# A fused attention, mixture-of-experts and MLP kernel: in each attention round x's copy goes first on ScalarE, then the state's copy and the first step on W, and W's raw pieces begin a round later

## The chip, the cores and the metric

The kernel runs on one core of a Trainium2 chip. The core has a matrix engine (TensorE, PE in the profile, with its weight loads as PEld), VectorE (DVE), ScalarE (ACT), GpSimd (POOL) and SyncE (SP), which here issues the transfers. Each engine runs its own instructions in program order, and the engines wait for one another by semaphores. The metric is the device time of one execution in microseconds.

## The reference: what is computed

Three stages follow one another. The first is a linear recurrence over 768 steps for 4 batches of 8 heads with 48 dimensions:

```python
cur = np.einsum('bhd,bhe->bhde', u[None] * kt, vt)
y[:, :, t] = np.einsum('bhd,bhde->bhe', rt, state + cur)
state = w[None, :, :, None] * state + np.einsum('bhd,bhe->bhde', kt, vt)
```

Its output, 3072 tokens of 384 numbers, is x. Tokens whose skip score is positive go to the best of 8 experts (a two-layer MLP, 384 to 1024 to 384), and their result is weighted and added. The last stage is `((x @ w1) * (x @ w2)) @ w3 @ w_out`. w3 and w_out don't depend on x, so the kernel forms their product W = w3 @ w_out once, while the recurrence runs.

## The kernel before

The recurrence is cut into 24 tiles of 128 tokens; a tile is a chunk of 64 steps for two of the batches, and two tiles (`bp` 0 and 1) make up a chunk of all four. The loop `for n in range(NT - 2)` (L807 to L847) issues one round for each tile. A round n computes the factors FK of tile n+2 (`prep`, DVE L384), the scores of tile n+1 (`scores`, PE L396), masks them into Fs (`evac`, DVE L401), puts the bonus on the diagonal (`bonus`: a reduce into z, DVE L420, and a copy_predicated into Fs, DVE L421), and then the output y of tile n (`y_mm`, PE L442 for the part inside the chunk and L445 for the state's part). y is copied to x (`x_out`, ACT L463) and stored; x of tile n-1 is transposed (`x_trans`, PE L473) and copied to xT (ACT L475), from which a round later the routing logits come (L486, L489). `ds_mm` (PE L458) adds to the state S, which stays in PSUM. `state_copy` multiplies S by the decay where a pair of chunks ends (DVE L430; tiles 4, 5, 8, 9, ...) and copies it to Ss (ACT L432) for the next y. z lies in the same PSUM bank as S, so the copy of S and the reduce into z are kept in the program's order. `prep_k` and `prep_m` (POOL L408, L414, L415) make kd and m.

Beside this, W is built. Its 13 jobs are four pieces of w_out (768 KB each) and eight of w3 (1024 KB each), in the order `o0, w3_0, o1, o2, o3, w3_1, ...`. The numbers come as 64-bit floats, read as pairs of 32-bit integers into `raww` (two buffers, L103, issued on SP), and are cut down to 32 bits. The generator `w_steps` (L657 to L713) gives three steps for a job: one with the join of job i (DVE L140), the issue of the load of job i+2 and the magnitude of job i+1 (ACT L111); one with the cast hi of job i (ACT L683) and low_bits of job i+1 (ACT L117); one with the remainder lo of job i (DVE L690) and signs of job i+1 (ACT L122). hi and lo are called wo_h, wo_l, w3h and w3l. PE's W matmuls (`keep`, L747) use them, and where there are none yet, dummy matmuls (L277) stand in their place.

The order is written by hand: the loop's body is the order of each engine, and the table `WN` says for each round how many of W's steps are taken at three places in it, the first at the round's top, the second behind x_trans, the third at the round's end. `fresh` is a list by which the kernel keeps, when the instructions are written out, which of W's pieces PE may use from which place of the program on. `state_copy` and the first of W's steps stand at the round's top, before scores; the first two raw loads are issued in rounds 0 and 1, each held until the mask of that round's scores (`copied`).

Of the kernel before, what the change touches and what calls it, by code (L numbers as in the profile page):

```python
# [15 lines left out]
ALU = mybir.AluOpType  # L16
# [4 lines left out]
P = 128  # L21
NB, NH, NS, HD = 4, 8, 768, 48
# [23 lines left out]
W3B = 3  # L46
NFIRST = 18
WK = [(1, 1)] * 9 + [(1, 2)] * 13
WN = [(0, 0, 0)] * 2 + [(1, 1, 1)] * 5 + [(1, 0, 1)] * 15
KW = 16  # L50
NRING = 8
RG = 3
# [11 lines left out]
def fused_kernel(ctx, tc, att, kv, wt, u, wg, we, w3, wo, w12, r, k, v, wu, out):  # L64
    nc = tc.nc
# [29 lines left out]
    def load_wide(pool, tag, src, ahead=2, gate=None):  # L95

        k = src.shape[1]
        if not wide:
            raw = pool.tile([P, k], F32, tag=tag, name=tag, bufs=ahead)
            dma = nc.sync.dma_start(out=raw, in_=src)  # L100
        else:
            raw = pool.tile([P, k, 2], I32, tag=tag, name=tag, bufs=ahead)
            dma = nc.sync.dma_start(out=raw.rearrange("p n w -> p (n w)"), in_=src.bitcast(I32))  # L103
        if gate:
            gate(dma)
        return raw
# [106 lines left out]
    def load_expert(e, q):  # L213
        raw = stg[(4 * e + q) % 3 // 2].tile([P, 2, 2 * D], F32, name="raw")
        nc.sync.dma_start(out=raw, in_=we[e, :, 2 * q:2 * q + 2, :])
        return raw
# [30 lines left out]
    with tc.manual_schedule():  # L247
# [6 lines left out]
        Ss = [ac.tile([P, NH, HD], F32, name=f"Ss{bp}") for bp in range(2)]  # L254
# [3 lines left out]
        def load_t(n):  # L258
            nc.sync.dma_start(out=TB[n % 3].rearrange("p a h t -> p (a h t)"), in_=att[n])
# [40 lines left out]
        def load_w(i, gate=None):  # L300
            if i < len(jobs):
                kind, q = jobs[i]
                raw_w.append(load_wide(nrp, "raww", wo[:, 2 * q * D:2 * q * D + 2 * D] if kind == "o" else w3[q], 2,
                                       gate and (lambda dma: behind(dma, gate, "transfers one after the other"))))
# [10 lines left out]
        for i in range(6):  # L315
            wn = pw[:, i - 1] if i else wc
            n = 1 << i
# [4 lines left out]
        w128 = pw[:, 6]  # L322
# [4 lines left out]
        S = [b[:, 0:D].rearrange("p (h d) -> p h d", h=NH) for b in SB]  # L327
# [52 lines left out]
        def prep(n):  # L380

            t = TB[n % 3]
            FK = FK_[n] = wk.tile([P, 2, NH, CH], F32, name="FK", bufs=3)
            return nc.vector.tensor_tensor(out=FK, in0=t, in1=UT[:, n // 2 % 2], op=ALU.mult)  # L384

        def behind(later, earlier, reason="two operands from SBUF each"):

            tc.add_manual_dep(later.ins, earlier.ins.name, mybir.DependencyInfo(
                mybir.DependencyClass.Sync, mybir.DependencyReason.DATA), reason=reason)

        def scores(n):
            FK = FK_[n]
            sc = ps_1.tile([P, 512], F32, tag="sc", name="sc").rearrange("p (h t) -> p h t", h=NH)
            for h in range(NH):
                for m, d in zip(half, dims):
                    nc.tensor.matmul(sc[m, h], FK[d, 1, h], FK[d, 0, h], start=True, stop=True)  # L396
            return sc

        def evac(n, sc):
            Fs = Fs_[n] = wk.tile([P, NH, CH], F32, name="Fs")  # L400
            return nc.vector.tensor_tensor(out=Fs, in0=sc, in1=mask[:, None, :].to_broadcast([P, NH, CH]), op=ALU.mult)  # L401

        def prep_k(n):

            c, bp = divmod(n, 2)
            if c < NC - 1:
                kd = kd_[n] = wk.tile([P, NH, HD], F32, name="kd")
                return nc.gpsimd.tensor_tensor(out=kd, in0=KV[bp][c % 2][:, 1], in1=KU[:, c % 2], op=ALU.mult)  # L408
# [9 lines left out]
        def bonus(n):  # L418
            z = SB[n % 2][:, 464 + NH * (n // 2 % 2):464 + NH * (n // 2 % 2) + NH]
            nc.vector.tensor_reduce(out=z, in_=P_.pop(n), axis=AX.X, op=ALU.add)  # L420
            nc.vector.copy_predicated(Fs_[n], diag[:, None, :].to_broadcast([P, NH, CH]).bitcast(I32),  # L421
                                      z[:, :, None].to_broadcast([P, NH, CH]))

        def state_copy(n):
            c, bp = divmod(n, 2)
            s = S[bp]
            if c == 0:
                return
            if c % 2 == 0:
                nc.vector.tensor_tensor(out=s, in0=s, in1=w128[:, :, None].to_broadcast([P, NH, HD]),  # L430
                                        op=ALU.mult)
            nc.scalar.copy(out=Ss[bp], in_=s)  # L432

        def y_mm(n, tag="y"):

            c, bp = divmod(n, 2)
            v, Fs, FK = KV[bp][c % 2][:, 2], Fs_.pop(n), FK_.pop(n)
            y = G if n % 2 and n < NT - 2 else ps_1.tile([P, 512], F32, tag=tag, name="y")
            yv = y[:, 0:D].rearrange("p (h d) -> p h d", h=NH)
            for h in range(NH):  # L440
                for m in half:
                    nc.tensor.matmul(yv[m, h], Fs[m, h], v[m, h], start=(h == 0), stop=True, skip_group_check=True)  # L442
            for h in range(NH if c else 0):
                for m, d in zip(half, dims):
                    nc.tensor.matmul(yv[m, h], FK[d, 0, h], Ss[bp][d, h], start=False, stop=True,  # L445
                                     skip_group_check=True)
            y_[n] = y
            if n < NT - 2:
                yb[0] = y
# [204 lines left out]
        done, fresh = set(), [[], [], []]  # L654
# [62 lines left out]
        def w_step(k):  # L717
            for _ in range(k):
                next(wprep, None)
# [10 lines left out]
        def w_ready():  # L730
            done.update(fresh[0])
            fresh[:] = fresh[1:] + [[]]
# [44 lines left out]
        sc = scores(0)  # L777
# [29 lines left out]
        for n in range(NT - 2):  # L807
            w_ready()
            if n == NT - 3:
                raws = {q: load_expert(0, q) for q in range(2)}  # L810
            fk = prep(n + 2)
            w_step(WN[n][0])
            state_copy(n + 1)
            sc = scores(n + 1)
            behind(prep_k(n + 1) or prep_m(n + 2), fk)
            if n < NT - 3:
                prep_m(n + 2)
            copied = evac(n + 1, sc)
            if n < 2:
                load_w(n, copied)  # L820
            bonus(n + 1)
            next(more_consts, None)
            w_ready()
            if n == 0:
                for _ in range(NFIRST):
                    dummy(DQ)
            y_mm(n)
            keep(4 * WK[n][0] if n else 0)
            run_todo()
            x_out(n)  # L830
            if n + 4 < NT:
                load_t(n + 4)
            if n > 0:
                x_trans(n - 1)
            keep(4 * WK[n][1] if n else 0)
            w_step(WN[n][1])
            w_evac(0)
            ds_mm(n)
            place_mm(n % 2)
            if n + 4 < NT:  # L840
                load_v(n + 4)
            if n < NT - 3:
                place(3)
            w_step(WN[n][2])
            run_todo(n < NT - 3)
            if n > 0:
                todo.append((logits, (n - 1,)))  # L847

        a, b, g = NT - 2, NT - 1, len(groups) - 1
        w_ready()  # L850
        sc = scores(b)
        todo.clear()
        yb[0] = G
        for i, step in enumerate([
                lambda: (state_copy(b), evac(b, sc), bonus(b), y_mm(a)),
                lambda: (x_trans(a - 1, G), x_out(a), logits(a - 2), route_a(g - 1)),
                lambda: (logits_out(a - 2), nc.scalar.copy(out=slots, in_=SL[1])),
                lambda: (y_mm(b, "sc"), logits(a - 1), route_b(g - 1), x_out(b)),
                lambda: (x_trans(a), logits_out(a - 1), route_c(g - 1)),
                lambda: (x_trans(b, SB[1]), place(4), place(4)),  # L860
                lambda: (logits(a), logits_out(a)),
                lambda: (logits(b), logits_out(b), route_a(g)),
                lambda: (route_b(g), place_rest()),
                lambda: place_all(g, nc.vector),
                lambda: [split_piece(0, q, raws[q // 2], nc.vector) for q in range(RG)]]):
            step()
            if i == 2:
                spare[0] = ps_1.tile([P, 512], F32, tag="y", name="spare")
            for _ in range(TP[i]):
                keep(TK[i])  # L870
                w_step(TW[i])
                w_ready()
                w_ready()
                if TE[i]:
                    w_evac(0)
# [636 lines left out]
```

## Time and profile before

| what | value |
|---|---|
| median of 3 runs | 632.18 us (631.43 to 632.35) |
| the profiled execution, its own time | 633.43 us |
| its span, first to last instruction | 631.7 us |
| mean granted clock of TensorE in it | 0.989 of full |
| PE busy | 609.8 us, 97% of the span |
| DVE busy | 455.6 us, 72% |
| ACT busy | 307.3 us, 49% |
| POOL busy | 141.4 us, 22% |

The span is what the trace holds; the execution's own time has some 1.7 us around it. Times in rows are microseconds from the span's start. PE's high share says little of any one place: it is an average over stages, and a matmul at the lower clock counts as busy too. The rounds of the loop lie between 13.76 and about 158 us.

### The profile page before, as it was taken

Reading aid. Unit: us, or ns where it says so; the run is one execution under the profiler, and the core shown is the slowest. Engines: PE = TensorE matmul, PEld = TensorE weight load, DVE = VectorE, ACT = ScalarE, POOL = GpSimd, SP = SyncE. Lnnn points to the kernel's source line nnn. Section 1 sums busy time; section 2 is a strip of 40 time slices with the busy share of each in tenths; the row PEclk is TensorE's granted clock in tenths of the full one; section 3 lists DMA queues with packets and bytes.
Section 4 is the critical chain, followed back from the end, with each engine's and each line's share of the span. In section 5 each row is a group of like instructions: output and inputs, shape, how many; then the busy total and the mean of one; then the engine's idle time right before and its main releaser. Section 6 shows DMA issues by size and latency. Waiting matters only on the chain.

```text
span 631.7 us, 15256 instructions
## 1 busy us (share of the span) xinstructions
PE 609.8 (97%) x6399; PEld 558.6 (88%) x6399; DVE 455.6 (72%) x807; ACT 307.3 (49%) x581; POOL 141.4 (22%) x143
## 2 busy tenths in 40 slices
PE   8899999999999999999999999999999999999996
PEld 7888889999889999899987989988988988988985
DVE  7676898988577799999956953854863863863770
ACT  1578877653256676666534543442443442442430
POOL 4954546463040232242132300000000000000000
PEclk9897999999999999999999999999999999999998
DMA  8989789766258778877321002002002002000001
GB/s 296 345 290 322 275 305 335 247 215 216 71 184 294 242 255 294 292 241 254 105 70 57 1 19 83 1 17 84 2 18 83 1 18 84 2 17 35 1 2 54
DMA packets 26940, 90.40 MB, mean 143 GB/s; under 512 B 4009, under 2 KB 10729, under 8 KB 25840
## 3 DMA queue, kind: packets, MB, share of 16 engines
q1 hardware_dynamic: 24816, 84.11, 38.5%
q0 software_dynamic: 2048, 5.24, 2.5%
q8 instruction: 52, 0.85, 0.5%
q14 instruction: 24, 0.20, 0.1%
HBM read 77.61 MB, written 12.39 MB: 142 GB/s over the span
## 4 chain that ended last, share of the span: by engine, by line
PE 71%; DVE 14%; DMA 6%; issue 4%; ACT 3%; POOL 1%; SPq 0%; DVEq 0%; ACTq 0%; POOLq 0%
PE po L1276 16%; PE xy L1235 11%; PE za L1235 10%; PE zb L1235 8%; PE hp L962 5%; PE y L981 4%; PE wp L747 3%; DVE elo L91 3%; PE sc L396 2%; PE S L458 2%; DVE hl L966 2%; DMA xr<-xm,sidx 1%; DMA raw<-in_w 1%; PE y L442 1%; DMA raww<-in_w 1%
## 5 line engine op out<-in xcount | busy, mean ns | idle before, releaser
L1217 DVE TENSOR_TENSOR C<-st,za 128x512 f32<-128x512 f32 x47 | 32.3, 688 | 69.7 <-ACT st L1252 69.6
L91 DVE TENSOR_TENSOR elo<-raw,ehi 128x768 fp32r<-128x768 f32 x64 | 60.4, 949 | 3.3 <-ACT ehi L90 3.3
L1276 PE MATMUL po<-pl,W_hi 128*128 128x512 f32 (+1 forms) x152 | 58.1, 383 | 0.0
L1276 PE MATMUL po<-ph,W_hi 128*128 128x512 f32 (+1 forms) x152 | 58.0, 381 | 0.0
L1276 PE MATMUL po<-ph,W_lo 128*128 128x512 f32 (+1 forms) x152 | 57.5, 379 | 0.0
L1252 ACT COPY st<-xy 128x256 f32<-128x256 f32 x47 | 17.6, 374 | 81.8 <-PE xy L1235 81.8
L962 PE MATMUL hp<-xh,ehi 128*128 128x240 f32 x192 | 54.4, 285 | 3.0 <-DVE hl L966 2.8
L90 ACT CAST ehi<-raw 128x768 fp32r<-128x768 f32 x64 | 52.6, 829 | 1.4 <-DMA raw<-in_we 1.4
L1235 PE MATMUL xy<-bxh,w12h 128*128 128x256 f32 x188 | 53.3, 283 | 0.0
L1235 PE MATMUL xy<-bxl,w12h 128*128 128x256 f32 x188 | 53.1, 282 | 0.0
L1235 PE MATMUL xy<-bxh,w12l 128*128 128x256 f32 x188 | 53.1, 282 | 0.0
L962 PE MATMUL hp<-xl,ehi 128*128 128x240 f32 x192 | 52.6, 276 | 0.0
L962 PE MATMUL hp<-xh,elo 128*128 128x240 f32 x192 | 52.3, 274 | 0.0
L1235 PE MATMUL za<-bxh,w12l 128*128 128x512 f32 x141 | 45.1, 320 | 0.0
L1235 PE MATMUL za<-bxh,w12h 128*128 128x512 f32 x141 | 45.0, 319 | 0.0
L1235 PE MATMUL za<-bxl,w12h 128*128 128x512 f32 x141 | 44.7, 317 | 0.0
L981 PE MATMUL y<-ehi,hh 128*128 128x384 f32 (+1 forms) x128 | 43.3, 339 | 0.0
L981 PE MATMUL y<-elo,hh 128*128 128x384 f32 (+1 forms) x128 | 43.2, 338 | 0.0
L981 PE MATMUL y<-ehi,hl 128*128 128x384 f32 (+1 forms) x128 | 43.1, 337 | 0.0
L962 PEld LDWEIGHTS hp<-xh,ehi 128*128 128x128 f32 x192 | 36.0, 189 | 7.7 <-DVE hl L966 7.2
L965 ACT ACTIVATE hh<-hp 128x240 fp32r<-128x240 f32 x64 | 23.7, 370 | 36.0 <-PE hp L962 35.9
L1000 POOL DMA_INDIRECT xm<-yo,sidx x16 | 21.8, 1359 | 84.7 <-DVE yo L997 53.8
(260 smaller groups left out, 1771.6 us busy)
## 6 DMA issues: line engine op xcount, KB each, us to landing
raw<-in_we SPq DMA_DIRECT2D x32, 768.0 KB, 5.2
KV<-in_kv SPq DMA_DIRECT2D x24, 576.0 KB, 5.8
TB<-in_att SPq DMA_DIRECT2D x24, 512.0 KB, 4.6
raww<-in_w SPq DMA_DIRECT2D x8, 1024.0 KB, 7.4
raw<-in_w SPq DMA_DIRECT2D x8, 768.0 KB, 6.9
xm<-xg SPq DMA_DIRECT2D x48, 96.0 KB, 2.9
out<-ob SPq DMA_DIRECT2D x17, 256.0 KB, 2.0
x<-xm SPq DMA_DIRECT2D x20, 192.0 KB, 2.7
```

Source lines behind the costliest of these rows:

```text
L90: nc.scalar.copy(out=hi, in_=raw)
L91: (eng or nc.vector).tensor_tensor(out=lo, in0=raw, in1=hi.bitcast(F32), op=ALU.subtract)
L396: nc.tensor.matmul(sc[m, h], FK[d, 1, h], FK[d, 0, h], start=True, stop=True)
L747: nc.tensor.matmul(ps, a[:, g], b[:, g], start=(g + i == 0), stop=(g == NF - 1 and i == 2))
L962: nc.tensor.matmul(hp, a, b, start=(i == 0), stop=(i == 8))
L965: nc.scalar.activation(out=hh, in_=hp, func=AF.Relu)
L981: nc.tensor.matmul(ys[e, t], a[:, P * t:P * t + ROWS[t]], b[:, D:2 * D], start=(f == 0 and i == 0), stop=(f == NF - 1 and i == 2))
L1000: ins = nc.gpsimd.indirect_dma_start(out=xm[:, :], out_offset=bass.IndirectOffsetOnAxis(ap=sidx[0:n, j, 1:2], axis=0), in_=yo, in_offset=N ...
L1217: nc.vector.tensor_tensor(out=halves(C[:, 0]), in0=st[:, 0:2], in1=halves(za), op=ALU.add)
L1235: nc.tensor.matmul(o, a, m, start=first and i == 0, stop=(i == 2), skip_group_check=True)
L1252: nc.scalar.copy(out=st[:, 0], in_=X)
L1276: nc.tensor.matmul(po, a[:, f, c], b[:, t], start=(i == 0), stop=(i == 3 * NF - 1))
```

## The change

The decay stays at the round's top as `state_decay`. The state's copy and W's first step move behind `x_out` and the issue of TB's load, ahead of `x_trans`. The first two raw loads are issued in rounds 1 and 2 instead of 0 and 1, and `WN` starts W's steps one step later; from round 8 on each step is in the same round as before. One line merges two entries of `fresh`, so that pieces finished at the new place count for PE from the same place as before.

```diff
@@ -46,7 +46,7 @@
 W3B = 3
 NFIRST = 18
 WK = [(1, 1)] * 9 + [(1, 2)] * 13
-WN = [(0, 0, 0)] * 2 + [(1, 1, 1)] * 5 + [(1, 0, 1)] * 15
+WN = [(0, 0, 0)] * 2 + [(0, 1, 1)] + [(1, 1, 1)] * 5 + [(1, 0, 1)] * 14
 KW = 16
 NRING = 8
 RG = 3
@@ -421,15 +421,16 @@
             nc.vector.copy_predicated(Fs_[n], diag[:, None, :].to_broadcast([P, NH, CH]).bitcast(I32),
                                       z[:, :, None].to_broadcast([P, NH, CH]))
 
+        def state_decay(n):
+            c, bp = divmod(n, 2)
+            if c and c % 2 == 0:
+                nc.vector.tensor_tensor(out=S[bp], in0=S[bp], in1=w128[:, :, None].to_broadcast([P, NH, HD]),
+                                        op=ALU.mult)
+
         def state_copy(n):
             c, bp = divmod(n, 2)
-            s = S[bp]
-            if c == 0:
-                return
-            if c % 2 == 0:
-                nc.vector.tensor_tensor(out=s, in0=s, in1=w128[:, :, None].to_broadcast([P, NH, HD]),
-                                        op=ALU.mult)
-            nc.scalar.copy(out=Ss[bp], in_=s)
+            if c:
+                nc.scalar.copy(out=Ss[bp], in_=S[bp])
 
         def y_mm(n, tag="y"):
 
@@ -809,15 +810,14 @@
             if n == NT - 3:
                 raws = {q: load_expert(0, q) for q in range(2)}
             fk = prep(n + 2)
-            w_step(WN[n][0])
-            state_copy(n + 1)
+            state_decay(n + 1)
             sc = scores(n + 1)
             behind(prep_k(n + 1) or prep_m(n + 2), fk)
             if n < NT - 3:
                 prep_m(n + 2)
             copied = evac(n + 1, sc)
-            if n < 2:
-                load_w(n, copied)
+            if 1 <= n < 3:
+                load_w(n - 1, copied)
             bonus(n + 1)
             next(more_consts, None)
             w_ready()
@@ -830,6 +830,9 @@
             x_out(n)
             if n + 4 < NT:
                 load_t(n + 4)
+            state_copy(n + 1)
+            w_step(WN[n][0])
+            fresh[-2:] = [fresh[-2] + fresh[-1], []]
             if n > 0:
                 x_trans(n - 1)
             keep(4 * WK[n][1] if n else 0)
@@ -852,7 +855,7 @@
         todo.clear()
         yb[0] = G
         for i, step in enumerate([
-                lambda: (state_copy(b), evac(b, sc), bonus(b), y_mm(a)),
+                lambda: (state_decay(b), state_copy(b), evac(b, sc), bonus(b), y_mm(a)),
                 lambda: (x_trans(a - 1, G), x_out(a), logits(a - 2), route_a(g - 1)),
                 lambda: (logits_out(a - 2), nc.scalar.copy(out=slots, in_=SL[1])),
                 lambda: (y_mm(b, "sc"), logits(a - 1), route_b(g - 1), x_out(b)),
```

On ACT this is round 3, from W's magnitude or x's copy to W's signs (in the rows, y and G are the outputs y of even and odd tiles, T the transposed x, Ss the copied state, narw and W the two places for W's 32-bit numbers; line numbers after the change are one higher). Before:

```order
L111 ACTIVATE narw<-raww 128x1024
L489 COPY L<-y 128x9
L683 CAST wo_h<-W 128x768
L117 ACTIVATE raww<-raww 128x1024
L432 COPY Ss_116<-S_203 128x384
L463 COPY xg<-G 128x384
L475 COPY xT<-T 128x384
L122 ACTIVATE raww<-raww 128x1024
```

After:

```order
L464 COPY xg<-G 128x384
L433 COPY Ss_116<-S_203 128x384
L111 ACTIVATE narw<-raww 128x1024
L476 COPY xT<-T 128x384
L684 CAST wo_h<-W 128x768
L117 ACTIVATE raww<-raww 128x1024
L122 ACTIVATE raww<-raww 128x1024
```

The copy of the state stood ahead of x's copy and behind W's cast and low_bits; it now follows x's copy at once. W's magnitude, which began the round, stands between it and xT, and the cast and low_bits stand behind xT.

On DVE, rounds 3 and 4, from one FK to the second next. Before:

```order
L384 TENSOR_TENSOR FK<-TB_120,UT 128x1024
L430 TENSOR_TENSOR S_203<-S_203,pw 128x384
L401 TENSOR_TENSOR Fs<-sc,mask 128x512
L420 TENSOR_REDUCE S_203<-m 128x8
L421 COPY_PREDICATED Fs<-diag,S_203 128x512
L690 TENSOR_TENSOR wo_l<-W,wo_h 128x768
L140 SCALAR_TENSOR_TENSOR narw<-narw,raww 128x1024
L384 TENSOR_TENSOR FK<-TB_118,UT 128x1024
L430 TENSOR_TENSOR S_204<-S_204,pw 128x384
L401 TENSOR_TENSOR Fs<-sc,mask 128x512
L420 TENSOR_REDUCE S_204<-m 128x8
L421 COPY_PREDICATED Fs<-diag,S_204 128x512
```

After:

```order
L384 TENSOR_TENSOR FK<-TB_120,UT 128x1024
L427 TENSOR_TENSOR S_203<-S_203,pw 128x384
L401 TENSOR_TENSOR Fs<-sc,mask 128x512
L420 TENSOR_REDUCE S_203<-m 128x8
L421 COPY_PREDICATED Fs<-diag,S_203 128x512
L140 SCALAR_TENSOR_TENSOR W<-W,raww 128x768
L691 TENSOR_TENSOR wo_l<-W,wo_h 128x768
L384 TENSOR_TENSOR FK<-TB_118,UT 128x1024
L427 TENSOR_TENSOR S_204<-S_204,pw 128x384
L401 TENSOR_TENSOR Fs<-sc,mask 128x512
L420 TENSOR_REDUCE S_204<-m 128x8
L421 COPY_PREDICATED Fs<-diag,S_204 128x512
```

Before, the join of a job stood at the round's top, ahead of FK, and lo behind the copy_predicated of the round after; now join and the lo of the same job both stand between copy_predicated and the next FK.

On SP, the issue order of the transfers from round 0 on (TB and KV are the attention's inputs, xm the stored x, raww W's raw pieces). Before:

```order
L103 DMA raww<-in_wo 128x1536
L466 DMA xm<-xg 64x384 x2
L259 DMA TB_119<-in_att 128x1024
L263 DMA KV_0_112<-in_kv 128x1152
L103 DMA raww<-in_w 128x2048
L466 DMA xm<-xg 64x384 x2
L259 DMA TB_120<-in_att 128x1024
L263 DMA KV_0_114<-in_kv 128x1152
L466 DMA xm<-xg 64x384 x2
L259 DMA TB_118<-in_att 128x1024
```

After:

```order
L467 DMA xm<-xg 64x384 x2
L259 DMA TB_119<-in_att 128x1024
L263 DMA KV_0_112<-in_kv 128x1152
L103 DMA raww<-in_wo 128x1536
L467 DMA xm<-xg 64x384 x2
L259 DMA TB_120<-in_att 128x1024
L263 DMA KV_0_114<-in_kv 128x1152
L103 DMA raww<-in_w 128x2048
L467 DMA xm<-xg 64x384 x2
L259 DMA TB_118<-in_att 128x1024
```

The first piece of w_out now comes behind the first TB and KV shown (tile 4), and the first piece of w3 behind the second ones (tile 5), where each stood ahead of them.

## Rows read from the trace of the kernel before

**Rows 1.** The page: PE's busy time, the granted clock by slices, W's raw loads.
```profile
PE 609.8 (97%) x6399; PEld 558.6 (88%) x6399; DVE 455.6 (72%) x807; ACT 307.3 (49%) x581; POOL 141.4 (22%) x143
...
PEclk9897999999999999999999999999999999999998
...
raww<-in_w SPq DMA_DIRECT2D x8, 1024.0 KB, 7.4
```

**Rows 2.** Windows by round: length, busy PE PEld DVE ACT POOL, clock, DMA, GB/s.
```profile
21.64:29.68 8.04, 6.67 (x151) 6.25 (x149) 4.51 (x5) 4.87 (x8) 7.75 (x14) 0.87 1.02 376
49.98:58.93 8.95, 8.95 (x145) 8.42 (x145) 7.00 (x9) 6.70 (x9) 2.98 (x3) 0.62 0.94 323
64.77:70.62 5.85, 5.85 (x149) 5.54 (x147) 5.72 (x10) 3.03 (x4) 3.83 (x3) 1.00 0.90 310
70.62:78.22 7.60, 6.65 (x161) 6.10 (x157) 5.11 (x11) 7.43 (x13) 4.07 (x3) 1.00 0.75 252
84.84:92.50 7.66, 7.01 (x149) 6.41 (x150) 7.60 (x10) 3.73 (x7) 4.82 (x5) 1.00 0.81 282
92.50:158.20 65.70, 65.70 (x1492) 62.17 (x1494) 57.77 (x104) 37.27 (x66) 33.97 (x30) 1.00 0.74 256
```

**Rows 3.** The chain of waits, 0 to 175 us: start, length, what.
```profile
26.17 1.37 issue
...
36.81 1.24 DVE narw L140
38.07 7.43 DMA raww<-in_wo
...
46.56 0.73 ACT wo_h L683
...
48.09 0.36 ACT Ss L432
...
48.84 0.38 ACT xT L475
...
51.06 0.97 DVE narw L140
...
59.64 0.87 ACT narw L111
...
63.10 0.57 DVE S L420
...
64.32 0.95 DVE wo_l L690
65.27 1.14 DVE FK L384
66.41 1.14 DVE narw L140
67.54 0.48 DVE S L430
68.02 0.57 DVE Fs L401
...
69.23 0.73 DVE Fs L421
```

**Rows 4.** The timeline, 29 to 52 us; in brackets idle time before, and releaser.
```profile
30.21 1.23 DVE L384 TENSOR_TENSOR FK<-TB,UT 128x1024 f32<-128x1024 f32 x1 [1.64 <-DMA TB<-in_att]
...
33.12 0.74 DVE L421 COPY_PREDICATED Fs<-diag,S 128x512 f32<-128x512 int32 x1
...
41.63 1.82 DVE L690 TENSOR_TENSOR w3l<-narw,w3h 128x1024 fp32r<-128x1024 f32 x1
...
45.58 0.93 ACT L111 ACTIVATE narw<-raww 128x768 f32<-128x768 f32 x1 [2.69 <-DMA raww<-in_wo]
...
48.56 0.56 DVE L420 TENSOR_REDUCE S<-m 128x8 f32<-128x384 f32 x1 [2.50 <-ACT Ss L432]
...
49.98 1.14 PE L442 MATMUL y<-KV,Fs 64*64 64x48 f32 x32 [1.52 <-ACT xT L475]
```

## Prediction

> **What bounds the kernel now.** I read the page first. PE is busy for 609.8 us of a 631.7 us span, and the line of granted clocks is below full in slices 2 to 4, the attention rounds alone [rows 1]. So only the rounds in which PE waits or runs slowly can give time back. Cut by round (I take a round to begin with its y matmuls, L442), the windows give the size: from 92.50 us on, PE is busy for 65.70 of 65.70 us, and round 8 shows what a round of PE work without a wait costs, 5.85 us [rows 2]. The rounds between 21.64 and 92.50 us are longer: round 2 takes 8.04 us, of which PE is idle 1.37 and runs at a granted clock of 0.87; round 6 takes 8.95 at 0.62; round 9 takes 7.60 with 0.95 idle [rows 2]. All granted clocks lie between two levels, 1.2 and 2.4 GHz, so 0.62 of 8.95 us is 6.8 us at the lower one, which costs half of that, 3.4 us; 0.87 of 8.04 us costs 1.0 us.
>
> The chain of waits tells what those rounds wait for. From 36.81 to 66.41 us it never touches PE: it goes join (DVE L140) to the raw load to ACT's pieces to the next join [rows 3]. The first turn lasts 51.06 - 36.81 = 14.25 us, the second 66.41 - 51.06 = 15.35 us, and each covers two rounds, because the raw tiles have two buffers and load i+2 waits for join i. So the kernel is bound here by a ring of about 7.1 to 7.7 us a round, against 5.85 of PE. The timeline shows how the ring reaches PE: in round 5 W's magnitude (ACT L111) waits 2.69 us for its raw load, the state's copy stands behind it on ACT, the reduce of z waits 2.50 us for that copy, and y(6) starts 1.52 us late [rows 4]. The profile names xT as y(6)'s releaser, but it had been written; the copy_predicated after that reduce is what came last.
>
> **The change part by part.** No operation is added or removed; PE and POOL keep their order. Four things move.
>
> (1) *The first two raw loads go a round later.* Ahead of the transfer TB(5), which FK(5) awaits for 1.64 us at 30.21 [rows 4], stood one 1,024 KB load that now comes behind it (the SP piece above). At the 376 GB/s of that stretch this is 2.8 us. The wait itself is all that FK(5) can gain at once: 1.64. The first join no longer stands before that FK either. So copy_predicated of round 3, which ended at 33.12 + 0.74 = 33.86, ends at about 32.2. Bounds: 33.86 if the load's place makes no difference, 31.0 if all of the 2.8 us shows. PE's idle 1.37 at 26.17, which the chain calls issue [rows 3], falls in the same crowded stretch (DMA share 1.02 [rows 2]); with or without it the scores of round 2 are done before that FK, so I give it nothing.
>
> (2) *x's copy and the state's copy go ahead of W's piece on ACT.* That takes the 2.50 us wait out of the reduce, since a late raw load no longer holds the state's copy, and it takes the state's copy, 0.36, and x's, which has the size of xT's 0.38, out of the old ring [rows 3]. What is now behind the waiting W piece on ACT: x's transposed copy (for whom PE's logits wait a round later), the cast hi, low_bits and signs.
>
> (3) *join and lo of a round both come after copy_predicated, and before the next FK.* This is the new cost. lo waits for the cast hi of the same round, hi stands behind xT and behind the magnitude that may wait for a load, and FK, decay, Fs, reduce and copy_predicated of the next round stand behind lo on DVE. So a one-round ring closes. By the chain's rows [rows 3]: Ss 0.36, magnitude 0.87, xT 0.38, hi 0.73, lo 0.95, FK 1.14, decay 0.48 (half of the rounds), Fs 0.57, reduce 0.57, copy_predicated 0.73: 6.78 with the decay, 6.30 without, either more than PE's 5.85. And the load's ring is still there, now through DVE: join 0.97, load 7.43, magnitude 0.87, xT 0.38, hi 0.73, lo 0.95, FK 1.14, Fs 0.57, reduce 0.57, copy_predicated 0.73: 14.34 us in two rounds, against 14.25 before. The old ring's tail (low_bits, Ss, xg, xT, signs) is exchanged for an equally long one.
>
> (4) *From round 8 on each step is in its old round.* Round 9, whose 0.95 us of idle the old order put behind signs, may lose it; xT now stands behind the piece there, which can cost the logits as much. I take both as nothing, with -1.6 to +1.6 as ends: the waits in rounds 9 and 11 sum to 1.6 (7.60 - 6.65 = 0.95 and 7.66 - 7.01 = 0.65 [rows 2]).
>
> **The sum.** Copy_predicated of round 3 ends at 32.2. To that of round 4: 6.78. Two turns of the load's ring lead to that of round 8: 14.34 and, with the 1,024 KB pieces and the decay, 15.35 as in the second turn before. That is 68.7, and y(9) can start 0.07 behind it: 68.7 against 70.62. I add one lo that is drawn out as the one at 41.63 of before was, 1.82 us [rows 4] where FK of the same 1,024 elements takes 1.14 [rows 3]: 0.68. So y(9) starts at 69.4, 1.2 us earlier, and from there on PE decides as before. The profiled execution took 633.43 us (its span of 631.7 and 1.7 around it): 633.43 - 1.2 = 632.2 us. The median of the runs shown is 632.18, so the profiled one was 1.25 above it, and the forecast is **no change: 632.2 us**. A measurement tells 0.2%, 1.26 us, from no change.
>
> Ends: the earliest copy_predicated (31.0), no stretched lo and the second turn at 14.34 + 0.48 give y(9) at 67.0, 3.6 earlier: 629.8. With copy_predicated at 33.86 and two stretched lo it is 71.8, 1.2 later: 634.6.
>
> **Rules beside rows.** PE's 1.37 us idle is followed at once by 1.2 GHz, and the 1.52 us before y(6) by the 6.8 us of it; the 0.95 us of round 9 is followed by full clock [rows 2 to 4]. The Trainium skill, "TensorE: Matmul & The Clock Gate", section "HAM oscillation", says that waits of PE for transfers, repeated in each iteration, let the clock fall again and again. The trace agrees as far as two such waits go. By that rule a kernel whose ring leaves a gap in every round, as this one's does, falls after the larger gaps: rival B.
> DVE's instructions with two operands are not always of one length: lo of 1,024 elements takes 1.82 us at 41.63, where POOL is at work beside it, and lo of 768 takes 0.95 at 64.32 [rows 3, 4]. The Trainium skill, "GPSIMD Engine Reference", section "Key points", has the two engines share their SBUF interfaces when a DVE instruction has two SBUF inputs. By it, a DVE that runs join, lo and FK in one piece would be met every round: all three lo that lie on the chain (rounds 3, 5 and 7) would be stretched, two more than the sum has, 1.4 us and 633.6 in all. One of the two rows speaks for it and one against, and I give it 0.06, within B's chance.
>
> **The rivals.**
> *A, faster.* The ring turns without collisions, and with the first loads out of the way neither the 1.37 us stall nor a fall of the clock occurs. For it: the two half-clock stretches of before cost 4.4 us between them, and both follow stalls in the stretch where loads crowd. Against: the ring, not PE, set rounds 3 to 8, so most of that was hidden under it. It gives the lower end, 633.43 - 3.6 = 629.8. Chance 0.29.
> *B, slower.* One place: y(7) or y(8), behind the magnitude that waits for its load in the ring of (3). Where PE idles there for 1.4 us or more, as before y(6), the clock falls, and a stretch like that of round 6 costs 3.4 us; the ring hides at most a third of it, since the stretch then reaches into rounds 9 and 10, where PE decides. That leaves 2.3 to 3.4: 632.2 + 2.6 = 634.8. It decides from a ring of 7.3 us a round on (5.85 + 1.45); the sum above has (14.34 + 15.35) / 4 = 7.4, but PE enters round 3 with some slack, as y(3) may start earlier, and the gaps spread over several rounds. Chance 0.32, with D and the rule on POOL in it.
> *C, no change by another way.* W's raw loads simply take as long as before, the DMA's 7.4 us [rows 1] set both rings, and the order on ACT is free. The median's 632.2 again; it is part of my forecast's chance.
> *D, W's parts come too late for PE.* PE's first W matmuls stand in round 6, and the parts for them are finished in rounds 3 and 4. A whole round of slack speaks against it; I give it 0.02.
>
> **How the numbers follow.** My forecast and C together have 0.39, A 0.29, B with D 0.32; these are also the chances for within 0.2%, faster and slower. The range must reach into A and B until a fifth is left out: from a little under A's 629.8, for a round 9 without its wait, 629.4, to 635.5, B with most of its price. The likeliest case alone has 631.0 to 633.5.
>
> **What would show it.** In the profile after, (1) is right if FK(5) starts before 29 us with no wait for TB. (2): no reduce waits for Ss longer than 0.5 us. (3): FK follows lo directly in rounds 4 to 8, the chain runs through join, load, hi, lo, FK and copy_predicated, and these rounds take 7.1 to 7.7 us each. (4): rounds 9 to 11 together lose 1 to 2 us. y(9) should start between 69 and 70 us. I am wrong if the rounds 3 to 8 come down to about 6 us (then the ring was not closed, A), if a half-clock stretch of over 3 us stands anywhere behind 55 us (B), or if the magnitude no longer waits for its loads at all.

## The result, and the profile after

The changed kernel took 635.81 us (median of 4 runs, 634.51 to 636.08) against 631.80 of before (4 runs, 631.25 to 632.35): 1.0058 of it, 95% interval 1.0037 to 1.0078. Repeated with 12 runs against 23, all on one chip, it was 634.25 against 632.74: 1.0029, interval 1.0007 to 1.0051. So the change makes the kernel slower, by 0.3 to 0.6%; the forecast was no change (632.2), and 635.81 lies 0.3 us above its range, 634.25 inside.

Page of the profiled execution after (634.51 us, span 632.8), the rows that answer to [rows 1]:

```profile
PE 610.3 (96%) x6399; PEld 558.9 (88%) x6399; DVE 457.7 (72%) x807; ACT 306.4 (48%) x581; POOL 143.5 (23%) x143
...
PEclk9979799999999999999999999999999999999999
```

Two dips of the clock, again before 92 us and in other slices. The windows by round, columns as in [rows 2]; here rounds 2, 4, 7, 8 and 9, and the later ones:

```profile
21.13:26.87 5.74, 5.74 (x152) 5.32 (x149) 3.22 (x5) 2.24 (x6) 5.53 (x11) 1.00 1.01 364
...
34.03:43.33 9.30, 8.19 (x153) 7.33 (x150) 7.16 (x9) 7.41 (x10) 5.22 (x4) 0.71 0.79 271
...
55.45:62.46 7.01, 6.22 (x149) 5.67 (x146) 4.46 (x7) 5.15 (x8) 2.59 (x4) 1.00 0.93 341
62.46:69.55 7.09, 6.26 (x143) 5.73 (x144) 5.18 (x8) 6.16 (x7) 3.78 (x4) 1.00 0.94 325
69.55:80.33 10.78, 9.75 (x154) 8.70 (x156) 9.07 (x16) 8.84 (x15) 3.76 (x4) 0.68 0.71 253
...
93.42:159.00 65.58, 65.25 (x1476) 61.61 (x1474) 58.48 (x104) 38.09 (x68) 32.18 (x30) 1.00 0.74 258
```

Round 2 has lost its wait and its slow stretch. Rounds 7 and 8 now take 7.0 and 7.1 us, round 4 9.30 (1.11 idle, clock 0.71) and round 9 10.78 (1.03 idle, clock 0.68).

The table of waits shows what was exchanged. First before, over rounds 2 to 11 (engine, tile and line that waited, for what; us in total, times, longest):

```profile
DVE S L420 <- ACT Ss L432: 5.5, 3, 2.5
...
ACT narw L111 <- DMA raww<-in_w: 2.7, 2, 1.8
ACT narw L111 <- DMA raww<-in_wo: 2.7, 1, 2.7
...
ACT W L111 <- DMA raww<-in_w: 2.6, 1, 2.6
```

and after:

```profile
DVE wo_l L691 <- ACT wo_h L684: 9.5, 4, 3.0
ACT Ss L433 <- DVE Fs L421: 7.4, 7, 2.2
...
DVE w3l L691 <- ACT w3h L684: 2.1, 1, 2.1
...
ACT W L111 <- DMA raww<-in_wo: 1.5, 1, 1.5
```

ACT's waits for raw loads, 9.3 us in all before (the three rows shown, and 1.3 in three waits for other pieces), are down to 1.5, and the reduce waits no more for Ss. In their place stand two that did not exist: Ss waits 7.4 us for copy_predicated, lo waits 11.6 for hi (9.5 and 2.1). ACT now waits for DVE in front of work that DVE waits for.

The chain of waits has that ring row by row, as the counterpart of [rows 3]:

```profile
58.84 1.22 DVE FK L384
...
61.63 0.74 DVE Fs L421
62.39 0.48 ACT Ss L433
62.87 1.05 ACT narw L111
63.93 0.36 ACT xT L476
64.29 0.74 ACT wo_h L684
65.09 0.84 issue
65.93 1.22 DVE FK L384
```

From FK at 58.84 to FK at 65.93 it is 7.09 us for one round, with the decay and the magnitude of a 1,024 KB piece; the prediction's terms give 6.78. What the chain calls issue ahead of the second FK is the time of lo, which takes 0.96 us from 65.06 on.

### The profile page after: what moved, and what is told of

Read it like the earlier page. It is cut to its first block, busy times and chain, and to the rows that moved or that the text cites. A ratio compares the mean times of both kernels' runs of the same rounds, so it can differ in the third digit from the quotient of the medians.

```text
span 632.8 us, 15244 instructions
## 1 busy us (share of the span) xinstructions
PE 610.3 (96%) x6399; PEld 558.9 (88%) x6399; DVE 457.7 (72%) x807; ACT 306.4 (48%) x581; POOL 143.5 (23%) x143
## 4 chain that ended last, share of the span: by engine, by line
PE 78%; DVE 11%; DMA 3%; issue 3%; ACT 2%; POOL 1%; SPq 0%; DVEq 0%; ACTq 0%; POOLq 0%
PE po L1279 16%; PE xy L1238 11%; PE za L1238 10%; PE zb L1238 8%; PE hp L965 6%; PE y L984 5%; PE wp L748 4%; DVE elo L91 3%; PE sc L396 3%; PE S L459 2%; PE y L443 1%; PE G L443 1%; PE y L446 1%; PE G L446 1%; DVE hl L969 1%
## 5 line engine op out<-in xcount | busy, mean ns | idle before, releaser
L965 PE MATMUL hp<-xh,ehi 128*128 128x240 f32 x192 | 54.5, 285 | 2.6 <-DVE hl L969 2.4
L1003 POOL DMA_INDIRECT xm<-yo,sidx x16 | 22.6, 1413 | 84.7 <-DVE yo L1000 58.6
```

Of the source, the lines that this page charges most:

```text
L965: nc.tensor.matmul(hp, a, b, start=(i == 0), stop=(i == 8))
L1003: ins = nc.gpsimd.indirect_dma_start(out=xm[:, :], out_offset=bass.IndirectOffsetOnAxis(ap=sidx[0:n, j, 1:2], axis=0), in_=yo, in_offset=N ...
```

## The experiments

Each time stands beside runs of the kernel before on the same chip; a ratio is to those. Runs of one kernel spread over some 6 us here, so the ratios carry the verdicts and the traces the mechanisms.

**The changed kernel again, twice, and the kernel before again.**

> The changed kernel once more, for its spread and a second trace. Three theories. Ring: the ring copy_predicated, Ss, magnitude, xT, hi, lo, FK, Fs makes rounds 6 to 8 seven us long, PE's scores wait 0.6 to 0.7 us for Fs in two of them, and the clock falls behind such gaps. State: in round 8 the copy Ss(9) stands on ACT behind the routing's r_d, so that y(9)'s second part starts 1.0 us late, and the clock falls there. Loads: it is the raw loads, now a round later. Expected by all: 635.8 us, 1.004 to 1.008 of before; y(12) between 93 and 96 us. By ring the scores' waits of 0.6 us or more stand in rounds 7 and 8 again, by state the wait of about 1.0 us before L446 in round 9.

> A third trace of the changed kernel. The sum of PE's waits in rounds 2 to 11 between 4 and 7 us, the clock's loss 3.4, 5.1 or 6.9 us; by state a wait before L446 in round 9 wherever PE reaches it on time; by ring gaps ahead of the scores in rounds 6 to 8.

> The kernel before, a second trace. If the falls of the clock lie at fixed places, at 28 and 51 us again; if they follow chance, elsewhere. Round 2's idle 1.4 us on PE is there again if it belongs to the order of this kernel.

The changed kernel took 634.25 us (12 runs), 635.01 in the single further run; before 633.61 in its single run. What all three theories expected, 635.8 us, 1.004 to 1.008 and y(12) between 93 and 96 us, was missed: it is 634.25 us, 1.0029 and, in the trace of that run, 91.28 us. That gives three traces after and two before. Times are told here from y(0), since the traces begin differently. Before, y(9) comes at 56.86 and 55.71 us, y(12) at 78.74 and 77.49. After, y(9) comes at 56.29, 55.65 and 54.54, y(12) at 80.16, 77.13 and 77.21. So at y(12) the two kernels stand level, at 78.1 us in the mean before and 78.2 after. From y(12) to the end of the span the third trace after takes some 2.8 us more than the other two; 1.49 us of that is one wait of PE in round 17 that the profile calls issue. The second trace of before, rounds 2 and 5:

```profile
21.91:27.78 5.87, 5.74 (x152) 5.32 (x149) 3.07 (x4) 3.72 (x5) 5.66 (x11) 1.00 1.01 372
41.19:50.95 9.76, 8.94 (x145) 7.95 (x147) 7.34 (x9) 6.69 (x9) 3.08 (x4) 0.65 0.78 255
```

Round 2 takes 5.87 us there without the 1.37 us wait and without a slow stretch, and the slow stretch lies in round 5. So the place of the falls, and the wait on which the prediction's reading of round 2 rested [rows 2, 3], change from one execution of the same kernel to the next and don't follow from its order alone. In the traces after, waits of 0.5 us or more before the scores for Fs stand in rounds 7 and 8 in two of three, the wait of 1.0 us before L446 of y(9) in two of three; where PE came late to y(9) for another reason, it was not there. PE's idle time in rounds 2 to 11 was 5.1, 4.3 and 6.0 us after, 5.3 and 5.0 before, and the clock's loss (length times one minus granted clock, by round) 6.9, 3.4 and 1.7 after, 5.1 and 3.4 before; the 6.0 us of waits in the third trace lie in the range that was expected, the 1.7 us do not.

By traces alone the two kernels can't be told apart; it takes the runs. There, the time times one minus the granted clock of each run is an estimate of what the clock takes: over 12 and 23 runs 5.0 us after and 5.2 before in the mean, and what is left is 629.4 against 627.6. **On that chip, by this estimate, the loss of 1.5 to 2 us is in waits and work at full clock, not in falls.** In the first 4 runs the clock took 7.6 us and 627.9 is left; the runs of before that stand beside them have no clock on record. Beside the 627.6 of the larger set those 4 runs point the other way, to falls, so what made up the first distance of 4.0 us isn't known.

**Half of the change: loads and W's steps later, order as before.**

```diff
-WN = [(0, 0, 0)] * 2 + [(1, 1, 1)] * 5 + [(1, 0, 1)] * 15
+WN = [(0, 0, 0)] * 2 + [(0, 1, 1)] + [(1, 1, 1)] * 5 + [(1, 0, 1)] * 14
-            if n < 2:
-                load_w(n, copied)
+            if 1 <= n < 3:
+                load_w(n - 1, copied)
```

> Only the loads and W's steps start later; ACT's order of a round and the place of state copy and of the first W step are those of before. Loads: 635 us or more. Ring and state: not slower than before, 631 to 633, since lo does not stand between hi of the same ring and FK, and Ss keeps its place ahead of r_d.

636.1 us, 1.0043 (1.0023 to 1.0063). By the time, Loads was right and ring and state were wrong. But the run doesn't show the loads apart from the order: the magnitude is now in front of Ss at the round's top, and waits there for its load:

```profile
ACT narw L111 <- DMA raww<-in_w: 5.1, 2, 3.0
...
ACT W L111 <- DMA raww<-in_w: 4.2, 2, 4.0
```

**The other half: the order alone, loads as before.**

```diff
-            if 1 <= n < 3:
-                load_w(n - 1, copied)
+            if n < 2:
+                load_w(n, copied)
...
-WN = [(0, 0, 0)] * 2 + [(0, 1, 1)] + [(1, 1, 1)] * 5 + [(1, 0, 1)] * 14
+WN = [(0, 0, 0)] * 2 + [(1, 1, 1)] * 5 + [(1, 0, 1)] * 15
```

> Only the order: state copy and the first W step behind x's copy, but loads and W's steps begin when they did before, so the first step is the cast hi and low_bits, and the magnitude stands at the round's end. Ring: without magnitude and xT between Ss and hi the ring is 1.2 us shorter, 5.6 plus join, some 6.2: 632 to 633.5. State: Ss(9) is still behind r_d, the wait of 1.0 us in round 9 stays and so does most of the loss: 634.5 to 636. Loads: as before, 631.8.

641.19 us, 1.0128 (1.0103 to 1.0153): all three theories missed. Rounds 4 and 5 take 9.9 and 9.8 us. I had summed the ring through lo and forgot the join, which in this order stands ahead of FK and waits for signs of the same round:

```profile
ACT Ss L433 <- DVE Fs L421: 22.1, 9, 3.6
...
PE sc L396 <- DVE Fs L401: 7.9, 6, 3.4
```

Ss 0.36, hi 0.73, low_bits 0.8, xT 0.4, signs 1.9 to 2.5, join 1.0, FK 1.1, Fs, reduce and copy_predicated 1.9 make 8.2 to 8.8 us. So each half alone loses more than both together: by the ratios 2.7 and 8.1 us against 1.8. Not all of the 8.1 is the ring itself: by the estimate above the clock takes 11.6 us in these runs, against 5.2 before, and in the trace rounds 4 and 5 lose 5.1 us to it, behind the wait of 3.4 us. Starting the loads a round later puts the magnitude, and not low_bits and signs, between Ss and the join; and the new place of W's step takes the late magnitude out from in front of Ss.

**The state's copy ahead of x's copy, and of the routing.**

```diff
             keep(4 * WK[n][0] if n else 0)
+            state_copy(n + 1)
             run_todo()
...
-            state_copy(n + 1)
             w_step(WN[n][0])
```

> The changed kernel with the state's copy issued ahead of the routing's work of the round (behind y's matmuls), so ahead of r_d and of x's copy; all else as changed. State: the wait before L446 in round 9 is gone, 632 to 633. Ring: the ring is the same, 635 to 636. Loads: 635 to 636.

639.17 us, 1.0096 (1.0070 to 1.0122). The wait before L446 in round 9 is gone, as State said, and the time is longer all the same; ring was not hard enough on it:

```profile
ACT Ss L433 <- DVE Fs L421: 22.6, 10, 6.1
DVE wo_l L691 <- ACT wo_h L684: 11.3, 4, 3.7
```

An Ss that comes earlier in ACT's order waits longer for copy_predicated (22.6 us, against 8.3 by the same window after), and x's copy, the magnitude and hi wait behind it.

**Without the edge from copy_predicated to Ss.**

```diff
-            z = SB[n % 2][:, 464 + NH * (n // 2 % 2):464 + NH * (n // 2 % 2) + NH]
+            z = wk.tile([P, NH], F32, name="z", bufs=2)
```

> The changed kernel with z in a small SBUF tile of its own instead of a column range of the state's PSUM bank, so that the state's copy need not wait for copy_predicated. Ring: the edge from copy_predicated to Ss closes the ring through ACT; without it what is left is join 0.97, hi 0.73, lo 0.95, FK 1.14, decay 0.48, Fs 0.57, reduce 0.57, copy_predicated 0.73, 5.7 to 6.1 us, near PE's pace: 1.5 to 3 us faster than the changed kernel, the wait of Ss for Fs gone. Loads: no difference (within 1 us of the changed kernel).

> The kernel before with z in SBUF. If the wait of the reduce for the state's copy behind a late magnitude was what bound it (5.5 us of waits in rounds 5 to 7), 1 to 2 us faster than before. If the ring through the raw load bound it whatever stands behind it, within 0.5 us.

639.05 us with the change, 1.0096 (1.0063 to 1.0129); 635.05 on the kernel before, 1.0030 (1.0005 to 1.0055). Neither the gains that were expected came, nor the equal times of the other theories. The wait of Ss is gone, but z's new place costs more than it gave. Groups of the changed kernel (busy us, mean ns of one, idle before):

```profile
L414 POOL TENSOR_TENSOR m<-KV,un 128x384 f32<-128x384 f32 x11 | 12.0, 1093 | 0.0
...
L421 DVE COPY_PREDICATED Fs<-diag,S 128x512 f32<-128x512 int32 x11 | 8.1, 736 | 0.4
...
L140 DVE SCALAR_TENSOR_TENSOR W<-W,raww 128x768 int32<-128x768 int32 (+1 forms) x4 | 4.3, 1072 | 1.3 <-ACT raww L122 1.3
```

and with z in SBUF:

```profile
L414 POOL TENSOR_TENSOR m<-KV,un 128x384 f32<-128x384 f32 x11 | 15.2, 1380 | 0.0
...
L421 DVE COPY_PREDICATED Fs<-diag,z 128x512 f32<-128x512 int32 x10 | 8.7, 865 | 0.3
...
L140 DVE SCALAR_TENSOR_TENSOR W<-W,raww 128x768 int32<-128x768 int32 (+1 forms) x4 | 5.7, 1422 | 1.2 <-ACT raww L122 1.2
```

copy_predicated takes 865 ns instead of 736, POOL's first product 1,380 instead of 1,093, the join 1,422 instead of 1,072. With z in SBUF a copy_predicated still takes 0.73 us where POOL stands still, and up to 1.14 us beside its products. The experiment took away a wait and added a collision, so it says nothing on the ring.

**lo a round later.**

```diff
-                nc.vector.tensor_tensor(out=lo, in0=x, in1=hi.bitcast(F32), op=ALU.subtract)
-                fresh[-1].append(jobs[i])
+                late.append((jobs[i], lo, x, hi))
+                if not wait_lo[0]:
+                    late_low(fresh[-1])
...
             state_copy(n + 1)
+            late_low(fresh[0])
             w_step(WN[n][0])
```

> The changed kernel with the remainder lo of rounds 3 to 7 a round later on DVE, behind the next copy_predicated and ahead of its join, so that no FK stands behind an instruction that waits for a cast of the same round. Ring: cut; DVE waits for ACT only at the join, rounds 3 to 8 at 5.9 to 6.5 us: 2 to 4 us faster than the changed kernel. Loads: the raw loads still come when they come, no difference within 1 us.

(wait_lo is set around the last step of rounds 3 to 7.) 633.6 us, 1.0026 (1.0004 to 1.0047), beside the changed kernel's 1.0029 and, in its first 4 runs, 1.0058. DVE's waits for ACT in rounds 2 to 11 fall from 12.9 us to 6.3, and the time stays. **So the ring through lo, though the chain shows it, is probably not what costs the most**: beside the larger set the 2 to 4 us that breaking it was to give back don't show, and Loads, which expected no difference, was right. Beside the first 4 runs some 2 us would show; the changed kernel was not run beside this one on the same chip, so this is not settled. PE's idle time in this trace is 5.3 us; what isn't put down to issue stands in rounds 8 to 11 now (0.70, 0.90, 0.86 and 0.33).

**The routing behind the copies, then r_d alone.**

```diff
             keep(4 * WK[n][0] if n else 0)
-            run_todo()
...
             state_copy(n + 1)
+            run_todo()
             w_step(WN[n][0])
```

> The changed kernel with the routing's work of a round (r_d and r_pr on ACT, their partners on DVE) issued behind x's copy and the state's copy instead of ahead of them; PE's order is the same. State: Ss(9) no longer waits for r_d, so no wait before L446 in round 9 or 10, and the changed kernel gains about 1 us of PE waits: 632.5 to 633.5 beside 634.4. If what the change costs lies in rounds 3 to 8, or is spread over many small waits, 634 to 635.

642.78 us, 1.0169 (1.0136 to 1.0203). The logits go with the routing, and they write into the PSUM bank that x's copy reads; issued behind it, they wait for it:

```profile
PE G L487 <- ACT xg L464: 3.7, 3, 2.3
PE y L487 <- ACT xg L464: 3.3, 1, 3.3
```

That spoils the test. The second one moves r_d alone, the other routing steps and the logits staying:

```diff
-            run_todo()
+            held = []
+            run_todo(hold=held)
...
             state_copy(n + 1)
+            for fn, args in held:
+                fn(*args)
+                todo.append((NEXT[fn], args))
             w_step(WN[n][0])
```

> The changed kernel with nothing moved but the routing's exponential r_d on ACT (rounds 8, 14, 18), from ahead of x's copy and the state's copy to behind them; PE, DVE and the logits stay as they were, which the earlier run on the routing did not leave. State: the wait of 1.0 us before L446 of y(9) is gone or under 0.5 us, and the time comes about 1 us nearer to before: 633 to 634 beside 634.4. Ring, or many small waits: that wait goes, but another takes its place by round 11; 634 to 635, the same as the changed kernel.

634.26 us, 1.0036 (1.0008 to 1.0064): no gain that shows, as Ring, or many small waits, had it. Its timeline:

```profile
70.00 0.48 ACT L433 COPY Ss<-S 128x384 f32<-128x384 f32 x1 [0.51 <-DVE Fs L421]
...
71.01 1.13 PE L446 MATMUL G<-Ss,FK 48*64 48x48 f32 x32
...
71.20 0.24 ACT L517 ACTIVATE r_d<-r_d 128x48 f32<-128x48 f32 x1 [0.73 <-DVE r_oh L516]
...
84.03 1.15 PE L396 MATMUL sc<-FK 48*64 48x64 f32 x32 [1.51 <-DVE Fs L401]
```

Ss(9) is copied ahead of r_d, and L446 in round 9 starts without a wait; in round 10 the scores wait 1.51 us for Fs instead. The wait behind r_d is real, and taking it away gave no time back. The three traces of the changed kernel have 0 to 0.74 us of idle PE in round 10; that the 1.51 us are the removed wait, moved on, is not shown.

**The state's copy ahead of W's piece, in the kernel before.**

```diff
-            w_step(WN[n][0])
             state_copy(n + 1)
+            w_step(WN[n][0])
```

> The kernel before with only the state's copy ahead of W's piece at the round's top. Before, cast and low_bits (1.5 us) and any wait in front of them stood ahead of the copy for which the reduce waits. If those waits bind (5.5 us of them in one trace before, 5.9 in the other), 630.5 to 632 beside 632.7. If the ring through the raw load sets the pace whatever stands in front of the reduce, within 0.5 us of before.

638.55 us, 1.0121 (1.0087 to 1.0156), again the other way than expected:

```profile
ACT Ss L432 <- DVE S L430: 8.8, 5, 2.3
```

The copy waits for the decay (DVE L430), and W's cast and low_bits, which before ran in that time, now stand behind it. That holds ACT up for 8.8 us (2.6 before), and the joins wait 6.0 us for signs (3.2 before). Yet this trace reaches y(12) at 78.31 us from y(0), no later than those before (78.74 and 77.49). What it lost lies behind the loop: some 5 us at 1.2 GHz between 160 and 180 us, slice 11 of its line of clocks. In the loop, a wait of 2.36 us in round 9 is followed by full clock:

```profile
PEclk9999999999699999999999999999999999999999
...
76.92 0.42 PE L458 MATMUL S<-KV,kd 64*48 64x48 f32 x9 [2.36 <-issue]
```

So that the copy's wait on ACT makes this kernel slower is not shown. Over its 6 runs the clock takes 9.9 us, against 4.7 in the runs before on that chip, and why is open. No kernel of the study beats the one before.

## Where the prediction was right and where it was wrong

**What held.** The ring of (2) and (3): the wait of the reduce for Ss is gone, FK follows lo, the chain runs through magnitude, xT, hi, FK, Fs and copy_predicated, and 7.09 us for a turn stand against 6.78 and, with loads, 7.4. The forecast for y(9), 69.4 - 13.76 = 55.6 us behind y(0), was met in the mean of three traces: 55.5, from 54.5 to 56.3. Rounds 3 to 8 of the profiled execution take 7.1 us in the mean, though singly from 5.9 to 9.3.

**Two of its signs did not hold.** FK(5) starts at 26.83, before 29 us, but still waits 1.12 us for TB. And a half-clock stretch of over 3 us behind 55 us, by which the prediction would call itself wrong and B right, stands in all three traces after: from 72 to 79 us in the profiled one, in round 7 of the second and in round 9 of the third, whose windows follow in this order:

```profile
53.58:63.58 10.00, 9.01 (x150) 8.40 (x147) 5.83 (x8) 7.28 (x12) 5.26 (x4) 0.67 0.92 318
...
68.28:77.56 9.28, 8.24 (x154) 7.23 (x156) 7.74 (x16) 8.15 (x14) 4.87 (x4) 0.82 0.62 216
```

**Two terms up to there were off and cancelled.** The timeline after, counterpart of [rows 4]:

```profile
26.83 1.59 DVE L384 TENSOR_TENSOR FK<-TB,UT 128x1024 f32<-128x1024 f32 x1 [1.12 <-DMA TB<-in_att]
...
29.99 0.73 DVE L421 COPY_PREDICATED Fs<-diag,S 128x512 f32<-128x512 int32 x1
...
33.47 1.75 POOL L415 TENSOR_TENSOR m<-KV,m 128x384 f32<-128x384 f32 x1
...
34.27 2.03 DVE L384 TENSOR_TENSOR FK<-TB,UT 128x1024 f32<-128x1024 f32 x1
```

Copy_predicated of round 3 ends at 30.72, that is 17.46 us behind y(0) (17.48 and 17.48 in the other traces) where the sum had 18.4 and the lower bound 17.2: step (1) was worth 2.6 us against the profiled execution and 2.1 against the second trace of before (19.60). In return FK(6) takes 2.03 us in all three traces, beside POOL's product L415, where 1.14 stood in the sum. The one drawn-out instruction that I took for lo is FK, so y(9) was met partly by luck. The Trainium skill, "GPSIMD Engine Reference", section "Key points", has POOL and VectorE share SBUF interfaces where a DVE instruction has two SBUF inputs; this trace agrees, 2.03 us for FK beside a product of POOL against 1.22 without one, and so does the run with z in SBUF. It isn't always DVE that is held: lo at 33.40 keeps its 0.96 us beside the same product, which takes 1.75 us instead of 1.00. The row that the prediction counted against this, lo at 64.32 before, has no product beside it; the last one ended at 63.18.

**The step that failed**, as far as the traces tell, is the one behind y(9): "from there on PE decides as before", with (4) taken as nothing. From y(9) to y(12) the traces before take 21.9 and 21.8 us, those after 23.9, 21.5 and 22.7, 0.8 more in the mean, in a range that I had put at 1.6 to either side and then set to zero. That takes back the 0.8 us by which these traces reach y(9) earlier than the two before (55.5 against 56.3): it accounts for the gain that didn't come, and the traces don't place the 1.5 us or more that were lost. The spread of the three, 2.4 us, is larger than that mean. A mechanism of it that I had not seen is Ss(9) behind r_d:

```profile
61.18 1.15 PE L396 MATMUL sc<-FK 48*64 48x64 f32 x32 [0.66 <-DVE Fs L401]
...
68.27 1.15 PE L396 MATMUL sc<-FK 48*64 48x64 f32 x32 [0.69 <-DVE Fs L401]
...
70.67 0.24 ACT L517 ACTIVATE r_d<-r_d 128x48 f32<-128x48 f32 x1 [2.03 <-DVE r_oh L516]
...
71.72 1.62 PE L446 MATMUL G<-Ss,FK 48*64 48x48 f32 x32 [1.03 <-ACT Ss L433]
```

Gaps of 0.66, 0.69 and 1.03 us follow in rounds 7 to 9, and the clock is at half from 72 to 79 us. That is rival B's place and price in this one execution. But B as a mechanism is not confirmed: in the third trace after, the same wait of 1.04 us was followed by 1.7 us lost to the clock in its round, and in the second there was no such wait. B's condition, a wait of 1.4 us or more, doesn't part the cases either, as a fall follows 1.03 us here and none the 2.36 us of the last experiment. And the clock's share is no larger than before in the larger set of runs, though it may be in the first 4. The chance for slower, 0.32, was given to falls of the clock; the larger set puts the loss into waits.

**The base was also off.** The sum was set against one execution, with a 1.37 us wait and two slow stretches that it took for the kernel's own. The second trace of before has neither at those places. A gain of 1.2 against an execution that is 1.25 above its median is no gain, which the prediction said; what it did not ask is whether the stall that it saw would come again.

**What stays open.** Three single edges were taken out of the changed kernel: lo ahead of FK, Ss behind r_d, and (with a side effect that spoils it) copy_predicated ahead of Ss. None gave the loss of the larger set back. Nor is there a run that moves the loads and leaves every other wait as it was: each half of the change alone has a wait of its own. Which of the remaining waits carries it isn't settled; that another wait stands behind a removed one, as in round 10 above, was seen, that this is the whole of it was not shown. That the distance was 4.0 us in the first comparison and 1.5 in the second is also open; the clocks of the two sets differ by 2.6 us (7.6 against 5.0).

## What to carry to other kernels

Moving a copy forward on an engine that runs in order helps only if its inputs are ready there: the changed kernel with Ss still further ahead stood 0.96% above the one before, against 0.29% without that move, and Ss held ACT up for 22.6 us instead of 8.3, in front of work that other engines needed. When a move closes a ring between two engines, sum the ring over every instruction between its ends on both, the ones that seem to belong to another step too; the kernel whose join I had left out of the sum stood 8 us above the one before, its falls of the clock included. And take a second trace before reading a stall of one trace as the kernel's own.

## Unexpected in the hardware

PE waits at fixed places of its program for nothing that the profile shows, in most of the kernels here. In the run that moves r_d alone:

```profile
32.48 0.87 PE L459 MATMUL S<-KV,kd 64*48 64x48 f32 x29 [1.07 <-issue]
...
38.41 0.38 PE L277 MATMUL wp<-zb 128*128 128x256 bf16 x2 [1.94 <-issue]
```

The wait ahead of the last 29 S matmuls of round 3 is there in 10 of 14 traces at 32.2 to 33.2 us, from 0.24 to 1.34 us long, and the one ahead of the last 2 dummies of round 4 in 12 of 14, from 0.18 to 2.17. The lengths change from one execution to the next of the same kernel (1.34, 0.79 and 1.25 after). How much of the spread between executions they make is not shown: the execution above, with 3.0 us of them, took 633.16 us, below the median of its kernel. What PE waits for there isn't known from these traces.
